# Three small changes at the hand-over from a dense stage to an expert stage: order of token-list loads, two more buffers for router rows, one group of matmuls moved

## The chip, the cores and the metric

The kernel runs on one core of one Trainium2 chip. The metric is the device time of one execution in microseconds (us). Engines: TensorE (PE, with its weight loads PEld), VectorE (DVE), ScalarE (ACT), GpSimd (POOL) and SyncE (SP), whose queue issues most DMAs; GpSimd issues the indirect ones.

## What is computed

Windowed causal attention (4 batches, 8 heads, 576 positions, head size 64), then a gated dense layer, then a top-1 routed layer of 8 experts. All is float32.

```python
attn = softmax(mask(q @ k.T / sqrt(D) + bias)); x = attn @ v        # 2304 tokens x 512
x = ((x @ w_a) * (x @ w_b)) @ w_out                                 # w_a, w_b: 512x1536, w_out: 1536x512
logits = x @ w_gate + modality_bias[modality_id]                    # 8 experts
e = argmax(logits); gate = max(softmax(logits))
out = gate * (relu(x @ w1[e]) @ w2[e])                              # w1[e]: 512x1024, w2[e]: 1024x512
```

## The kernel before

**Dense stage.** Tokens are cut into 18 tiles of 128 rows, in seven chunks of 3, 2, 2, 3, 3, 3 and 2 tiles (`CH`). A chunk runs 12 steps `j`; each has two accumulations of 12 matmuls (`mm_ab`, L503: `x @ w_a` and `x @ w_b`), the product of the two on DVE (`gf`, L1174), its split into two parts on ACT and DVE (`g`), and, one step later, the matmuls with `w_out` (`mm_out`, L520). Float32 accuracy comes from splitting each operand into a rounded part and a rest and adding three products. The order on PE, ACT and DVE is the written one in this stage (`tc.manual_schedule`); elsewhere a scheduler decides it.

**Router.** For chunks 2 to 5 the eight logits of a tile are taken on DVE during the next chunk: `rd_dot(e)` (L599) multiplies the three tiles of the chunk by row `e` of the gate matrix (`wgt`, 128x512, broadcast to all partitions, 256 KB) and sums (L602, tile `junk`). `rd_fetch(e)` (L594) asks for a row. There are two row buffers: rows 0 and 1 are asked for ahead of the chunk, row `e + 2` behind `rd_dot(e)`. For the last chunk (6), whose steps are `step6`, these dots run in its first eight steps. ACT and DVE have another duty in these steps: the first weights of the first expert unit (`un0`, a unit whose expert is known early) are loaded in quarters (`w1_load`, L893) and split (`w1_split`, L886 on ACT, L887 on DVE).

**Hand-over.** After the last chunk PE runs the first unit's first product (GEMM1, tile `ps_h`, L1282, 32 groups of three matmuls, each group one `yield` of `u_big`). Its groups are used to fill the gaps of a chain of small steps: transposes and logits of the last two tiles (`ps_x`, `ps_l`), their ranks (`ps_r`), the counts of tokens (`ps_c`, `ps_d`, `ps_e`) and the values `uv` that say which expert and which token list each later unit takes. The tables `AE` and `AD` say how many groups stand behind each of these steps: `AD[6]` first, then `AE` after each of the six parts of the last tiles' routing, then `AD[3]`, `AD[4]`, `AD[5]` behind `ps_c`, `ps_d`, `ps_e`, then all that is left.

**Expert stage.** Five units (`NFIX`) of 384 tokens follow for certain (`big(u)`), with one small unit inside the third. A unit's token list (`idx`, three columns of 128 numbers, a DMA of single numbers issued by SP, `u_idx`, L916) is needed by three indirect gathers on POOL (`xg`, L927), which bring 384 rows of 513 floats from the table `x2d`. PE transposes them (`ps_t`, L944), ACT and DVE split the result (`xT`). Eight weight quarters of 512 KB (`wr`: four of `w1`, four of `w2`) are asked for by SP through four buffers, and split by ACT and DVE into `w1s` and `w2s`. Then come GEMM1 (96 matmuls, `ps_h`) and GEMM2 (72 matmuls, `ps_y`, L1265). The scheduler places the transposes of a unit among the GEMM2 matmuls of the unit before. SP issues in order, and so does POOL.

Here unit 0 of this loop is called U0; the unit ahead of it, which runs GEMM1 in the hand-over and GEMM2 behind it, is called UE. In the code before, the lists of U0 and the four units behind it are asked for ahead of U0's weights.

Of the kernel before, what the change touches and what calls it, by code (L numbers as in the profile page):

```python
# [7 lines left out]
F32 = mybir.dt.float32  # L8
# [8 lines left out]
P = 128  # L17
# [4 lines left out]
def attn_moe_moe2(ctx: ExitStack, tc, q, k, v, moe_w_a, moe_w_b, moe_w_out, modality_id,  # L22
                  w_gate, w_gate_t, modality_bias, w1, w2, out):
    nc = tc.nc
    N, DM = out.shape
    DFF = moe_w_out.shape[0]
    E = w_gate.shape[1]
# [28 lines left out]
    m1 = ctx.enter_context(tc.tile_pool(name="m1", bufs=2))  # L56
# [54 lines left out]
    RG = N + 3 * P  # L111
    UT = 3 * P
    NSLOT = N // UT
    NS = E * NSLOT
    NFIX = N // UT - 1
    HT = P // 2
    NBIG = 11
# [314 lines left out]
    def wab_load(j):  # L432
        r = wab_p.tile([P, 2, KD, P, 2], U32, tag=f"wab{j}", name=f"wraw{j}")
        for m, w in enumerate((moe_w_a, moe_w_b)):
            nc.sync.dma_start(out=r[:, m].rearrange("p k f t -> p (k f t)"), in_=w.bitcast(U32)[j])
        wraw[j] = r
# [25 lines left out]
    def wo_load(j):  # L462
        r = m1.tile([P, DM, 2], U32, tag="wo", bufs=WOB, name="wor")
        mark["wo"] = nc.sync.dma_start(out=r.rearrange("p a b -> p (a b)"),
                                       in_=moe_w_out.bitcast(U32)[j * P:(j + 1) * P, :]).ins
        wraw["o", j] = r
# [122 lines left out]
    wgt = {}  # L589
# [3 lines left out]

    def rd_fetch(e):  # L594
        if not wgt:
            wgt[0] = m1.tile([P, 2, DM], F32, tag="ff", bufs=1, name="wgt")
        nc.sync.dma_start(out=wgt[0][:, e % 2], in_=w_gate_t[e:e + 1].partition_broadcast(P))

    def rd_dot(e):  # L599
        for i, x2, lgr in now:  # L600
            junk = m1.tile([P, DM], F32, tag="x2T", bufs=1, name="junk")
            nc.vector.tensor_tensor_reduce(out=junk, in0=x2[:, 0:DM], in1=wgt[0][:, e % 2], scale=1.0, scalar=0.0,  # L602
                                           op0=ALU.mult, op1=ALU.add, accum_out=lgr[:, e:e + 1])
        if e + 2 < E:
            rd_fetch(e + 2)

    def rd_step(j):
        if now and DJ <= j < DJ + E:
# [49 lines left out]
    @hp  # L658
    def a_loads(g):
        while pos["load"] < len(plist) and first[plist[pos["load"]]] <= g:  # L660
            c, hp = plist[pos["load"]]
            pairs[c, hp] = a_load(c, hp)
            pos["load"] += 1
# [216 lines left out]
    def ld(tile_, col, hi):  # L880
        return nc.values_load(tile_[0:1, col:col + 1], engines=SP, min_val=0, max_val=hi,
                              skip_runtime_bounds_check_because=WHY)

    def split(dst, srcw, early=False):
        if not early:
            nc.scalar.copy(out=dst[:, 0], in_=srcw)  # L886
            nc.vector.tensor_tensor(out=dst[:, 1], in0=srcw, in1=dst[:, 0], op=ALU.subtract)  # L887
            return
        for k in range(srcw.shape[1]):
            nc.scalar.copy(out=dst[:, 0, k], in_=srcw[:, k])  # L890
            (nc.gpsimd if k < W2P else nc.vector).tensor_tensor(out=dst[:, 1, k], in0=srcw[:, k], in1=dst[:, 0, k], op=ALU.subtract)

    def w1_load(ev, pool, f):  # L893
        r = pool.tile([P, KD, 2 * P], F32, tag="wr", name="wr1")
        nc.sync.dma_start(out=r.rearrange("p k f -> p (k f)"), in_=w1[bass.ds(ev, 1), f].rearrange("o p x -> p (o x)"))
        return r

    def w1_split(r):
        t = w1p.tile([P, 2, KD, 2 * P], F32R, tag="w1", name="w1s")
        split(t, r)  # L900
        return t

    def u_w1(ev, pool):
        return [w1_split(w1_load(ev, pool, f)) for f in range(4)]

    def u_w2(ev, pool, early=False):
        W2 = []
        for f in range(4):
            r = pool.tile([P, 2, DM], F32, tag="wr", name="wr2")
            nc.sync.dma_start(out=r.rearrange("p k f -> p (k f)"),  # L910
                              in_=w2[bass.ds(ev, 1), f].rearrange("o p x -> p (o x)"))
            t = w2p.tile([P, 2, 2, DM], F32R, tag="w2", name="w2s")
            split(t, r, early)
            W2.append(t)
        return W2

    def u_idx(ov, nt, pool, tag="idx", bufs=2):
        idx = pool.tile([P, 3], I32, tag=tag, bufs=bufs, name="idx")
        nc.sync.dma_start(out=idx[:, :nt], in_=tab[bass.ds(ov, nt * P), 0:1].rearrange("(t p) o -> p (t o)", p=P))
        return idx  # L920
# [232 lines left out]
    def evac(c):  # L1153
        for _ in evac_out(c):
            pass
        tr[:] = [[0, r] for r in tr]
        now.extend(rd)
        rd.clear()
# [46 lines left out]
    for c in range(NC):  # L1205
        n = CH[c] * P
        for j in range(NJ):
            if c == 0:
                if j == 0:
                    pe.enter_context(tc.manual_schedule(engines={  # L1210
                        mybir.EngineType.PE, mybir.EngineType.Activation, mybir.EngineType.DVE}))
                if j == 0:
                    wab_load(4)
                if j != 1:
                    wo_load(max(j, 1))
                if 0 < j < NJ - 4:
                    with tc.issue_after(mark["wo"]):
                        wab_load(j + 4)
                if j == CJ:
                    with tc.issue_after(mark["pt"]):  # L1220
                        consts_b()
                a_loads(goal[j] + LDA)
                pend, sc, tp = step0(j, pend, sc, tp) if j else step00()
                continue
            if j == 0:
                if c == NC - 1:
                    assert not sc and not tp and cur["s"] == len(items)
                    at_st.close()
                    w1p = ctx.enter_context(tc.tile_pool(name="w1p", bufs=4, side="right"))
                    wrp = ctx.enter_context(tc.tile_pool(name="wrp", bufs=1, side="right"))  # L1230
                    xgp = ctx.enter_context(tc.tile_pool(name="xgp", bufs=1, side="right"))
                if c - 1 in RD:
                    rd_fetch(0)
                    rd_fetch(1)
                mm_out(*pend, *([wo_t[NJ - 1]] if c == 1 else []))
                pend = None
                if c == 1:
                    evac(c - 1)
            if c > 1:
                wo_fetch(j, c)  # L1240
            if c < NC - 1:
                a_loads(goal[c * NJ + j] + LDA)
                if c == 3 and (j == 5 or j > 5 and zr):
                    x2_init()
                pend, sc, tp = step(c, j, pend, sc, tp)
                continue
            pend = step6(j, pend)
# [5 lines left out]
    m2 = ctx.enter_context(tc.tile_pool(name="m2", bufs=1))  # L1253
# [41 lines left out]

    fin = ExitStack()
    fin.enter_context(tc.manual_schedule(engines={mybir.EngineType.PE}))
    AD = [0,0,0,3,4,5,5]
    AE = [2,2,2,3,4,2]
    mm_out(*pend)  # L1300
    adv(AD[6])
    for a, _ in zip(AE, evac_out(NC - 1)):
        adv(a)
# [4 lines left out]
    nc.tensor.matmul(ps[:NS, 0:1], lhsT=os6.rearrange("p m e -> p (m e)"), rhs=ones[:, 0:1], start=True, stop=True)  # L1308
    adv(AD[3])
    un = rt.tile([P, 16], F32, tag="un", bufs=1, name="un")  # L1310
# [10 lines left out]
    nc.tensor.matmul(ps2[:NS, 4:7], lhsT=ones[:NS, :NS], rhs=ab[:NS, 0:3], start=True, stop=True)  # L1321
    adv(AD[4])
    nc.vector.tensor_copy(out=u_[:, 4:7], in_=ps2[:NS, 0:3])
# [20 lines left out]
    nc.tensor.matmul(ps3[0:1, :], lhsT=onef[:NS], rhs=vt[:NS], start=True, stop=True)  # L1344
    adv(AD[5])
    uv = const.tile([1, NV + 4], I32, name="uv")
# [89 lines left out]
            out=out, out_offset=bass.IndirectOffsetOnAxis(ap=idx, axis=0),  # L1436
            in_=y[0:HT], in_offset=None, bounds_check=N - 1, oob_is_err=False))

    S_A, S_B, S_C = 20, 29, 4

    def big(u, after=None, cont=None):
        ev = ld(uv, u, E - 1)
        pool = side()
        idx, xg = u_gather(*((None, 3, pool, idxs[u]) if u < NFIX else (ld(uv, NBIG + u, E * RG - UT), 3, pool)))
        W1, W2 = u_w1(ev, wrq), u_w2(ev, wrq)
        if after is not None:
            gs = small_load(after)
        xT = u_xT(xg, 3, pool, m_bank)
        for n_, _ in enumerate(u_big(idx, xg, xT, W1, W2, m_bank, FO and u != NFIX - 1)):
            if after is not None and n_ in (S_A, S_B):  # L1450
                next(gs)
            if cont is not None and n_ == S_C:
                next(cont, None)
        return gs if after is not None else None
# [6 lines left out]
    def small(u):  # L1461
        for _ in small_load(u):
            pass


    idxs = [u_idx(ld(uv, NBIG + u, E * RG - UT), 3, m2, f"idx{u}", 1) for u in range(NFIX)]
    gs = None
    for u in range(NFIX):
        gs = big(u, 0 if u == SAT - 1 else None, gs)
# [61 lines left out]
```

## Time and profile before

| | us |
|---|---|
| median of 3 runs (829.09 to 830.67) | 829.64 |
| the profiled execution: its own time | 828.1 |
| its span, first to last instruction | 826.4 |
| PE busy in the span | 800.0 (97%) |
| PEld, DVE, ACT, POOL busy | 721.9, 546.0, 460.7, 231.8 |

A row of the time-ordered view gives the start, the length, the engine, the line, the operation with its output and inputs, and in brackets how long the engine stood idle before it and who released it. Names are those of the program, without buffer numbers.

### The profile page before, as it was taken

Reading aid. Unit: us, or ns where it says so; the run is one execution under the profiler, and the core shown is the slowest. Engines: PE = TensorE matmul, PEld = TensorE weight load, DVE = VectorE, ACT = ScalarE, POOL = GpSimd, SP = SyncE. Lnnn points to the kernel's source line nnn. Section 1 sums busy time; section 2 is a strip of 40 time slices with the busy share of each in tenths; the row PEclk is TensorE's granted clock in tenths of the full one; section 3 lists DMA queues with packets and bytes.
Section 4 is the critical chain, followed back from the end, with each engine's and each line's share of the span. In section 5 each row is a group of like instructions: output and inputs, shape, how many; then the busy total and the mean of one; then the engine's idle time right before and its main releaser. Section 6 shows DMA issues by size and latency. Waiting matters only on the chain.

```text
span 826.4 us, 14380 instructions
## 1 busy us (share of the span) xinstructions
PE 800.0 (97%) x4686; PEld 721.9 (87%) x4686; DVE 546.0 (66%) x1571; ACT 460.7 (56%) x1161; POOL 231.8 (28%) x365
## 2 busy tenths in 40 slices
PE   9979999999999999999999999999998999999994
PEld 6857877998999999999999999989987998989893
DVE  7789997777666776668777776378746444446510
ACT  7755547877778766676667643223526444557420
POOL 5324261433243322342223322020422030303101
PEclk9999999999999999999999999999999999999997
DMA  9956646677556866555556444475438554638301
GB/s 244 372 197 213 231 139 194 216 225 228 172 161 176 224 170 171 143 152 144 158 149 170 126 134 121 132 228 206 142 104 278 194 182 131 214 92 316 120 14 41
DMA packets 78629, 145.13 MB, mean 176 GB/s; under 512 B 14095, under 2 KB 41903, under 8 KB 78544
## 3 DMA queue, kind: packets, MB, share of 16 engines
q1 hardware_dynamic: 74992, 134.39, 53.5%
q0 software_dynamic: 3552, 9.73, 3.3%
q8 instruction: 39, 0.64, 0.3%
q14 instruction: 46, 0.38, 0.1%
HBM read 118.16 MB, written 22.12 MB: 170 GB/s over the span
## 4 chain that ended last, share of the span: by engine, by line
PE 57%; issue 16%; DVE 11%; ACT 8%; DMA 4%; POOL 3%; SPq 0%; POOLq 0%; ACTq 0%
PE ps_ab L503 27%; PE acc L520 10%; PE ps_h L1282 5%; PE ps_y L1265 3%; PE acc L516 3%; PE ps_o L378 2%; PE ps_s L258 2%; ACT p L282 2%; PE ps_p L310 1%; POOL out L1272 1%; DVE f64f L426 1%; POOL xg L927 1%; DVE junk L602 1%; DMA xg<-x2d,idx 1%; DMA wgt<-in_wgt 1%
## 5 line engine op out<-in xcount | busy, mean ns | idle before, releaser
L503 PE MATMUL ps_ab<-xr,wab 128*128 128x384 f32 (+1 forms) x2016 | 326.5, 316 | 3.1 <-DVE gf L1174 1.3
L503 PEld LDWEIGHTS ps_ab<-xr,wab 128*128 128x128 f32 x2016 | 307.1, 188 | 14.9 <-issue 4.3
L520 PE MATMUL acc<-wo,g 128*128 128x512 f32 x540 | 135.3, 393 | 0.0
L326 POOL TENSOR_SCALAR_AFFINE_SELECT pt<-pc 128x512 fp32r<-128x512 f32 (+1 forms) x72 | 46.6, 647 | 268.6 <-DVE pc L324 243.8
L520 PEld LDWEIGHTS acc<-wo,g 128*128 128x128 f32 x540 | 96.9, 188 | 16.8
L1282 PE MATMUL ps_h<-xT,w1s 128*128 128x384 f32 x576 | 104.4, 337 | 0.0
L1265 PE MATMUL ps_y<-w2s,h 128*128 128x512 f32 x432 | 104.3, 396 | 0.0
L1282 PEld LDWEIGHTS ps_h<-xT,w1s 128*128 128x128 f32 x576 | 99.8, 188 | 0.9
L1265 PEld LDWEIGHTS ps_y<-w2s,h 128*128 128x128 f32 x432 | 80.7, 190 | 15.8
L282 ACT ACTIVATE p<-p,mx 128x128 f32<-128x128 f32 x144 | 56.8, 395 | 29.6 <-DVE mx L272 29.4
L602 DVE CUSTOM_DVE_ANT_0 junk<-x,wgt 128x512 f32<-128x512 f32 x88 | 62.0, 704 | 4.2 <-DMA wgt<-in_wgt 2.2
L387 ACT COPY u<-ps_o 64x384 f32<-64x384 f32 x120 | 56.8, 473 | 7.6 <-PE ps_o L378 6.2
L1272 POOL DMA_INDIRECT out<-y,idx x18 | 20.1, 1116 | 138.2 <-ACT y L1271 136.9
L301 ACT ACTIVATE p<-p,mx 128x128 f32<-128x128 f32 x120 | 41.8, 395 | 26.4 <-DVE mx L290 26.2
L1116 ACT CAST g<-gf 128x384 fp32r<-128x384 f32 (+1 forms) x60 | 28.2, 470 | 50.5 <-DVE gf L1114 50.0
L1117 DVE TENSOR_TENSOR g<-gf,g 128x384 fp32r<-128x384 f32 (+1 forms) x60 | 30.3, 505 | 37.7 <-ACT g L1116 37.7
L887 DVE TENSOR_TENSOR w2s<-wr,w2s 128x1024 fp32r<-128x1024 f32 x24 | 29.4, 1225 | 36.8 <-ACT w2s L886 35.8
L1114 DVE TENSOR_TENSOR gf<-ps_ab,asb 128x384 f32<-128x384 f32 (+1 forms) x60 | 30.2, 503 | 32.6 <-PE ps_ab L503 24.2
L887 DVE TENSOR_TENSOR w1s<-wr,w1s 128x1024 fp32r<-128x1024 f32 x28 | 34.2, 1224 | 23.4 <-ACT w1s L886 22.3
L1285 ACT ACTIVATE h<-ps_h 128x384 fp32r<-128x384 f32 x48 | 23.5, 491 | 40.8 <-PE ps_h L1282 38.7
L328 POOL TENSOR_SCALAR_AFFINE_SELECT pt<-pc 128x512 fp32r<-128x512 f32 (+1 forms) x72 | 46.3, 642 | 0.0
L1286 DVE SCALAR_TENSOR_TENSOR h<-ps_h,h 128x384 fp32r<-128x384 f32 x48 | 26.3, 554 | 24.9 <-ACT h L1285 24.8
(218 smaller groups left out, 1204.9 us busy)
## 6 DMA issues: line engine op xcount, KB each, us to landing
wo<-wo_d SPq DMA_DIRECT2D x60, 512.0 KB
wr<-in_moe_w SPq DMA_DIRECT2D x56, 512.0 KB
wgt<-in_wgt SPq DMA_DIRECT2D x32, 256.0 KB
wraw<-in_moe_w_a SPq DMA_DIRECT2D x12, 512.0 KB
wraw<-in_moe_w_b SPq DMA_DIRECT2D x12, 512.0 KB
wor<-in_moe_w_out SPq DMA_DIRECT2D x12, 512.0 KB
wo_d<-wo SPq DMA_DIRECT2D x12, 512.0 KB
kr<-in_k SPq DMA_DIRECT2D x24, 256.0 KB
```

The source lines that it names most:

```text
L282: nc.scalar.activation(out=it.p[:, h, :], in_=it.p[:, h, :], func=AF.Exp, bias=it.mx[:, 2 + h:3 + h], scale=-1.0, accum_out=it.mx[:, 4 + h ...
L301: nc.scalar.activation(out=it.p[:, h, :], in_=it.p[:, h, :], func=AF.Copy, scale=it.mx[:, 6 + h:7 + h])
L326: nc.gpsimd.affine_select(out=it.pt[:, :, 0], in_=pc, pattern=pat + [[-1, P]], base=0, channel_multiplier=1, compare_op=ALU.is_gt, fill=0.0)
L328: mark["pt"] = nc.gpsimd.affine_select(out=it.pt[:, :, 1], in_=pc, pattern=pat + [[1, P]], base=0, channel_multiplier=-1, compare_op=ALU.i ...
L387: nc.scalar.copy(out=u[o:o + 64], in_=it.po[o:o + 64, 1 - h:4 - h])
L503: nc.tensor.matmul(ps[:, :n], lhsT=w[:, m, r, kk * P:(kk + 1) * P], rhs=xr[:, s, kk, :n], start=(idx == 0), stop=(idx == len(terms) - 1))
L520: nc.tensor.matmul(acc[c, t], lhsT=g[:, r, t * P:(t + 1) * P], rhs=w[:, s, :], start=(j == 0 and idx == 0), stop=(j == NJ - 1 and idx == 2))
L602: nc.vector.tensor_tensor_reduce(out=junk, in0=x2[:, 0:DM], in1=wgt[0][:, e % 2], scale=1.0, scalar=0.0, op0=ALU.mult, op1=ALU.add, accum_ ...
L887: nc.vector.tensor_tensor(out=dst[:, 1], in0=srcw, in1=dst[:, 0], op=ALU.subtract)
L1117: nc.vector.tensor_tensor(out=gt[:, 1, :n], in0=gf[:, :n], in1=gt[:, 0, :n], op=ALU.subtract)
L1265: nc.tensor.matmul(pss[t], lhsT=h[:, r, f, t * P:(t + 1) * P], rhs=W2[f // 2][:, s_, f % 2, :], start=(f == 0 and i == 0), stop=(f == 7 an ...
L1282: nc.tensor.matmul(ps, lhsT=W1[f // 2][:, r, kk, (f % 2) * P:(f % 2 + 1) * P], rhs=xT[:, s_, kk, :], start=(kk == 0 and i == 0), stop=(kk ...
```

## The change

1. `rd_fetch` and `rd_dot` take the row buffers from a dictionary, and in the last chunk two more are added (`w6`, in a pool that opens on the space of the attention buffers when these close). So four rows are asked for at the start of that chunk, and row `e + 4` behind `rd_dot(e)`.
2. `AE` goes from `[2,2,2,3,4,2]` to `[2,2,3,3,3,2]`; of `AD`, entry 4 goes from 4 to 5 and entry 5 from 5 to 4. The sums are the same.
3. The list of U0 is asked for alone; those of units 1 to 4 are asked for in `big(0)`, behind the requests for U0's eight weight quarters.
4. `S_B`, which says in which group of the third unit a part of the small unit is written, goes from 29 to 30.

```diff
     def rd_fetch(e):
         if not wgt:
-            wgt[0] = m1.tile([P, 2, DM], F32, tag="ff", bufs=1, name="wgt")
-        nc.sync.dma_start(out=wgt[0][:, e % 2], in_=w_gate_t[e:e + 1].partition_broadcast(P))
+            ff = m1.tile([P, 2, DM], F32, tag="ff", bufs=1, name="wgt")
+            wgt.update({0: ff[:, 0], 1: ff[:, 1]})
+        nc.sync.dma_start(out=wgt[e % len(wgt)], in_=w_gate_t[e:e + 1].partition_broadcast(P))
...
-        if e + 2 < E:
-            rd_fetch(e + 2)
+        if e + len(wgt) < E:
+            rd_fetch(e + len(wgt))
...
+                    w6 = xgp.tile([P, 2, DM], F32, tag="wgt", name="wgt")
+                    wgt.update({2: w6[:, 0], 3: w6[:, 1]})
                 if c - 1 in RD:
-                    rd_fetch(0)
-                    rd_fetch(1)
+                    for e in range(max(2, len(wgt))):
+                        rd_fetch(e)
...
-    AD = [0,0,0,3,4,5,5]
-    AE = [2,2,2,3,4,2]
+    AD = [0,0,0,3,5,4,5]
+    AE = [2,2,3,3,3,2]
...
-    S_A, S_B, S_C = 20, 29, 4
+    S_A, S_B, S_C = 20, 30, 4
...
         W1, W2 = u_w1(ev, wrq), u_w2(ev, wrq)
+        if u == 0:
+
+            lists(range(1, NFIX))
...
-    idxs = [u_idx(ld(uv, NBIG + u, E * RG - UT), 3, m2, f"idx{u}", 1) for u in range(NFIX)]
+    idxs = {}
+
+    def lists(us):
+        for u in us:
+            idxs[u] = u_idx(ld(uv, NBIG + u, E * RG - UT), 3, m2, f"idx{u}", 1)
+
+    lists((0,))
```

**SP, start of the last chunk.** The three stores of the chunk before to the table, then the loads of `w_out` parts. Before:

```order
L561 DMA x2d<-x_6257 128x513
L483 DMA wo<-wo_d 128x1024 x4
L881 TENSOR_LOAD uv_663
L919 ISA
L919 DMA idx<-tab 128x3x1
L881 TENSOR_LOAD uv_663
L895 ISA
L895 DMA wr_7255<-in_moe_w 128x1024
L483 DMA wo<-wo_d 128x1024
L597 DMA wgt<-in_wgt 128x512
```

After:

```order
L561 DMA x2d<-x_6257 128x513
L598 DMA wgt<-in_wgt 128x512 x2
L483 DMA wo<-wo_d 128x1024 x4
L882 TENSOR_LOAD uv_663
L920 ISA
L920 DMA idx<-tab 128x3x1
L882 TENSOR_LOAD uv_663
L896 ISA
L896 DMA wr_7258<-in_moe_w 128x1024
L483 DMA wo<-wo_d 128x1024
L598 DMA wgt<-in_wgt 128x512
```

Two router rows (2 and 3) now stand ahead of the `w_out` loads; the next request, at the same place as before, is for row 4 where it was for row 2. The last two requests of the chunk are gone.

**SP, behind the counts.** `uv` names the unit's expert and list. Before, the fifth list, with four alike ahead of it, and then the first weight quarter:

```order
L881 TENSOR_LOAD uv
L919 ISA
L919 DMA idx<-tab 128x3x1
L881 TENSOR_LOAD uv
L895 ISA
L895 DMA wr_8315<-in_moe_w 128x1024
```

After, the first list is followed at once by the weights, and the other four stand behind the eighth quarter:

```order
L882 TENSOR_LOAD uv
L920 ISA
L920 DMA idx<-tab 128x3x1
L882 TENSOR_LOAD uv
L896 ISA
L896 DMA wr_8296<-in_moe_w 128x1024
```

Four list requests with their register loads have left the place between U0's list and its weights.

**PE, from the counts to the first product of U0.** Before:

```order
L1321 MATMUL ps_d<-ab,ones 48x3
L1282 MATMUL ps_h<-xT,w1s 128x384 x12
L1344 MATMUL ps_e<-vt,onef 1x40
L1282 MATMUL ps_h<-xT,w1s 128x384 x15
L1265 MATMUL ps_y<-w2s,h 128x512 x28
L944 MATMUL ps_t<-ident,xg 128x128 x4
L1265 MATMUL ps_y<-w2s,h 128x512
L944 MATMUL ps_t<-ident,xg 128x128 x4
L1265 MATMUL ps_y<-w2s,h 128x512 x42
L1282 MATMUL ps_h<-xT,w1s 128x384 x96
```

After:

```order
L1324 MATMUL ps_d<-ab,ones 48x3
L1285 MATMUL ps_h<-xT,w1s 128x384 x15
L1347 MATMUL ps_e<-vt,onef 1x40
L1285 MATMUL ps_h<-xT,w1s 128x384 x12
L1268 MATMUL ps_y<-w2s,h 128x512 x46
L945 MATMUL ps_t<-ident,xg 128x128 x4
L1268 MATMUL ps_y<-w2s,h 128x512 x6
L945 MATMUL ps_t<-ident,xg 128x128 x8
L1268 MATMUL ps_y<-w2s,h 128x512 x20
L1285 MATMUL ps_h<-xT,w1s 128x384 x96
```

One group of three stands ahead of `ps_e` now and not behind it. The transposes of U0's rows, in thirds of four, stand behind 46, 52 and 52 products of UE's GEMM2; they stood behind 28, 29 and 30. On ACT and DVE the splits of these transposes (`xT`) come after all four quarters of `w1` now, where they came after two. The change of `S_B` moves nothing on PE.

## Rows read from the trace of the kernel before

**Rows 1.** Stretches: busy us (count) of PE, PEld, DVE, ACT, POOL; clock, DMA share, GB/s
```profile
core 0: us, PE busy (x) PEld busy (x) DVE busy (x) ACT busy (x) POOL busy (x), PEclk, DMA share, GB/s
589.90:611.80 21.90, 21.08 (x130) 19.42 (x129) 16.26 (x69) 10.02 (x23) 8.15 (x7) 1.00 0.32 116
611.80:634.50 22.70, 19.44 (x86) 15.80 (x85) 9.77 (x11) 10.64 (x14) 4.92 (x5) 0.92 0.80 249
651.20:669.10 17.90, 17.90 (x86) 14.76 (x86) 7.51 (x9) 7.67 (x11) 0.31 (x1) 1.00 0.36 124
```
**Rows 2.** Time-ordered view, last chunk: SP, DVE, PE and ACT around a router row
```profile
520.21 1.51 SPq L561 DMA_DIRECT2D x2d<-x  x3
543.15 0.38 SPq L597 DMA_DIRECT2D wgt<-in_wgt  x1
547.19 0.42 SPq L597 DMA_DIRECT2D wgt<-in_wgt  x1
549.64 0.34 SPq L895 DMA_DIRECT2D wr<-in_moe_w  x1
555.08 0.69 DVE L602 CUSTOM_DVE_ANT_0 junk<-x,wgt 128x512 f32<-128x512 f32 x1 [2.16 <-DMA wgt<-in_wgt]
557.64 1.70 PE L503 MATMUL ps_ab<-xr,wab 128*128 128x256 f32 x12 [1.04 <-DVE gf L1174]
557.93 1.04 ACT L886 CAST w1s<-wr 128x1024 fp32r<-128x1024 f32 x1
562.23 0.42 DVE L1174 TENSOR_TENSOR gf<-ps_ab,asb 128x256 f32<-128x256 f32 x1
```
**Rows 3.** Time-ordered view, hand-over: the two waits of PE
```profile
598.00 1.06 PE L540 MATMUL ps_l<-wg,x2T 128*128 128x8 f32 x8 [0.37 <-ACT x2T L535]
608.94 0.23 PE L1344 MATMUL ps_e<-vt,onef 48*1 48x40 f32 x2 [0.45 <-DVE vt L1340]
```
**Rows 4.** Time-ordered view behind the counts: lists and weights on SP, gathers on POOL
```profile
609.95 3.93 SPq L919 DMA_DIRECT2D idx<-tab  x5
614.63 2.60 SPq L895 DMA_DIRECT2D wr<-in_moe_w  x4
612.61 0.97 POOL L927 DMA_INDIRECT xg<-x2d,idx  x1 [7.25 <-DMA idx<-tab]
615.15 0.95 POOL L927 DMA_INDIRECT xg<-x2d,idx  x1 [0.30 <-issue]
636.99 1.48 POOL L927 DMA_INDIRECT xg<-x2d,idx  x1 [0.30 <-issue]
638.77 0.97 POOL L927 DMA_INDIRECT xg<-x2d,idx  x1 [0.30 <-issue]
```
**Rows 5.** Time-ordered view, PE in GEMM2 of UE
```profile
619.57 0.66 PE L944 MATMUL ps_t<-ident,xg 128*128 128x128 f32 x4 [0.58 <-DMA xg<-x2d,idx]
623.15 1.12 PE L944 MATMUL ps_t<-ident,xg 128*128 128x128 f32 x4 [2.68 <-DMA xg<-x2d,idx]
```
**Rows 6.** Chain of waits, in order of time: start, us, what (GEMM1 of U0, then GEMM2)
```profile
634.69 16.67 PE ps_h L1282 x96
...
663.22 5.93 PE ps_y L1265 x26
```
**Rows 7.** One stretch of 1 us, columns as in rows 1
```profile
624.00:625.00 1.00, 1.00 (x5) 0.81 (x4) 0.79 (x2) 1.00 (x4) 0.00 (x0) 0.50 1.00 344
```
**Rows 8.** DMA view by stretch: 613.5:615, 617:623, 618:620, 547:554 (software = gathers): packets, MB
```profile
q0 software_dynamic: 26, 0.11, 49.5%
...
q1 hardware_dynamic: 454, 1.68, 75.5%
q0 software_dynamic: 143, 0.46, 24.5%
...
q0 software_dynamic: 25, 0.07, 9.7%
...
q0 software_dynamic: 266, 0.79, 36.2%
```

More of the change, by code (lines that the diff above doesn't have):

```diff
@@ L601, in rd_dot @@
             junk = m1.tile([P, DM], F32, tag="x2T", bufs=1, name="junk")
-            nc.vector.tensor_tensor_reduce(out=junk, in0=x2[:, 0:DM], in1=wgt[0][:, e % 2], scale=1.0, scalar=0.0,
+            nc.vector.tensor_tensor_reduce(out=junk, in0=x2[:, 0:DM], in1=wgt[e % len(wgt)], scale=1.0, scalar=0.0,
                                            op0=ALU.mult, op1=ALU.add, accum_out=lgr[:, e:e + 1])
-        if e + 2 < E:
-            rd_fetch(e + 2)
+        if e + len(wgt) < E:
+            rd_fetch(e + len(wgt))
     def rd_step(j):
```

## The prediction

> **What bounds the kernel now.** I read the table of engines first: PE is busy for 800.0 of 826.4 us, so the end is set by PE's work, and a change of order can win only where PE stands still or runs slowly. The table by slices and then the stretches show where that is. Between 611.8 and 634.5 PE does 86 matmuls in 22.70 us and is busy for 19.44 of them; between 651.2 and 669.1 it does the same mix, 86 matmuls, in 17.90 us without a gap [rows 1]. The first of these is GEMM2 of UE with the transposes of U0, the second GEMM2 of U0 with the transposes of the next unit. The time-ordered view names the wait: the second and third set of transposes wait 0.58 and 2.68 us for gathered rows [rows 5]. The stretch view adds a second loss. Right behind the wait the granted clock is 0.50, that is 1.2 GHz instead of 2.4, while PE is busy for the whole microsecond [rows 7]; ahead of it PE had stood from 620.5 to 623.15. So the slow stretch is part of the price of the wait: 22.70 - 17.90 = 4.8 us in all, 3.26 of it standing (22.70 - 19.44) and some 1.5 slow.
>
> Two smaller losses stand ahead of it. In the last chunk DVE waits 2.16 us for a router row, and PE then 1.04 us for `gf`, which stands behind that dot on DVE [rows 2]. In the hand-over PE waits 0.37 us for `x2T` and 0.45 for `vt` [rows 3].
>
> **Part 1, router rows.** The row that came too late was asked for at 547.19 and was there at 555.08, 7.9 us later [rows 2]. With four buffers it is asked for behind the stores of the chunk before, which are issued from 520.21 to 521.7, more than 30 us before its dot. Row 4 is then asked for at 543.15, where row 2 was, and its dot runs after 557, so it has 14 us where 7.9 were needed. The two early requests stand ahead of four loads of `w_out` on SP. They carry 0.5 MB and take two issue times of about 0.4 us [rows 2]; the loads behind them serve steps from 540 on, so 15 us and more hide this. The new buffers lie where the attention's buffers were, so the requests wait for the last attention work; the first `w_out` load behind that is issued before 522, and I cost the wait at nothing with the same cover. No bytes are added: eight rows before, eight after.
>
> What is late next? On ACT the split of a weight quarter (`w1s`, 557.93) follows. It was asked for at 549.64 [rows 2], and nothing shows when it landed. Its DVE half, three dots and the next `gf` (562.23) follow in order, and that `gf` is only just in time for PE now. For the whole 1.04 to stay won, the quarter must land by 556.9, 1.04 before the split's present start. By the 7.9 us of the router row it lands at 557.5, and 0.5 us are won; by its place in the queue, two requests and 0.5 MB behind the row that was there at 555.08, at 0.36 MB per us (2.14 MB from 617 to 623 [rows 8]), it lands at 556.5, and 1.04 are won. If it landed only at 557.9, nothing is won. I take **0.8**, between the two nearest, and keep 0 and 1.04.
>
> **Part 2, one group of matmuls.** A group is three matmuls at 16.67 / 96 = 0.17 us, or 0.52 us [rows 6]. One more stands ahead of the second `ps_l`, where PE waited 0.37, and one more ahead of `ps_e`, where it waited 0.45 [rows 3]; both are covered. Against it, one fewer stands ahead of the second tile's ranks and one fewer behind `ps_e`. The first takes 0.52 us of cover from DVE's steps for the second tile; at worst all of it comes back as a wait, and 0.82 - 0.52 = 0.3 are left. The second has the whole of GEMM2 behind it and costs nothing. I take **0.7**, since no wait of PE for these ranks shows in the trace; bounds 0.3 and 0.82.
>
> **Part 3, lists and transposes.** Before, SP issues five lists from 609.95 to 613.9 and the first weight quarter of U0 at 614.63 [rows 4]. Without four lists, at about 0.9 us each, the quarters start near 610.8. The first gather waits for its own list alone and stays at 612.61. The moved lists stand behind the eighth quarter, whose issue waits for the splits of the first four; the next unit's gathers started at 636.99 [rows 4], behind a scatter on POOL, so the list has some ten microseconds to spare, and SP's next work (the weights of the next unit) waits for buffers then anyway.
>
> What removes the wait is mainly the order on PE. GEMM2 of UE now starts one group earlier, 611.8 - 0.5 = 611.3. The first third of the transposes stands behind 46 products of 5.93 / 26 = 0.228 us [rows 6], at 611.3 + 10.5 = 621.8, and the last two thirds behind six more and four transposes, at about 623.7. Before, the last rows were there at 623.15 [rows 5], so even an unchanged landing is in time. But the landing does change: the weights now flow beside the gathers from their first byte, where they came two microseconds later.
>
> How long do the gathers take then? They move 384 x 513 x 4 bytes = 0.79 MB, and their first bytes show between 613.5 and 615 [rows 8], say 614.3. The gathers of UE, in a stretch with some weight traffic, moved their 0.79 MB in 7 us (547 to 554); beside U0's weights the same queue moved 0.46 MB in 6 us (617 to 623) [rows 8], which would make 10.3 us. So the last row lands between 621.3 and 624.6; the middle, 622.9, is ahead of 623.7. I take no wait, so the stretch takes the 17.90 us of its twin and **4.8** are won; at 624.6 PE waits 0.9 and 3.9 are won.
>
> Two rules of the Trainium skill bear on this. The rows show that the gather queue got 143 packets against 454 of the weights from 617 to 623 [rows 8]. DMA: Bandwidth & Descriptors, section Queues, rings and completion order, says that a DMA engine serves its queue rows in turn, a packet each; by even turns the gathers would get about half of 0.36 MB per us and land near 618.7. The trace does not agree that far, and its shares stand in the sum. The other speaks against the change. A gather issued at 636.99, beside a weight split on DVE, took 1.48 us on POOL, the next 0.97 [rows 4]. SBUF — State Buffer, section SBUF: two separate sides, says that a VectorE operation with two SBUF inputs can hold a port pair that GpSimd then waits for. By it the first splits of U0, which now come earlier, delay the third gather (615.15) by up to 0.5 us; the slow bound becomes 625.1, the wait 1.4, and the sum 0.5 lower there.
>
> The change of `S_B` moves nothing on PE; nothing.
>
> **Sum.** 0.8 + 0.7 + 4.8 = 6.3 us. The profiled execution took 828.1 us (826.4 and 1.7 around it), so it would be 821.8; it stands 1.5 under the median of 829.64, from which I subtract the same: **823.3 us**.
>
> **Rivals.**
> - *The gathers get thin beside the weights* (0.15): they land between 624.6 and 627, PE waits 1 to 3.3 us, and the clock falls again in the longer cases. For it speaks that the gather queue's share fell to 0.07 MB in 2 us from 618 to 620 [rows 8]; against it that these were the worst two microseconds. At 627 all of the 4.8 is back (3.3 standing, 1.5 slow): 829.6 - 1.5 = 828.1. The case runs from 824.3 to 828.1.
> - *The router row's wait is taken over by the weight quarter* (0.10): it lands at 557.9, part 1 gives nothing, 829.6 - 5.5 = 824.1. For it speaks the 7.9 us of the row asked just before.
> - *The gathers starve, and the kernel gets slower* (0.05): at 0.035 MB per us, the rate of 618 to 620 [rows 8], 0.79 MB take 22.5 us and land at 636.8; PE waits 13.1, the slow clock adds 1.5, and this loss of 14.6 stands where 4.8 was: 829.6 + 9.8 - 1.5 = 837.9. It decides from a landing at 630.2, a rate under 0.05: then the loss of 8.0 exceeds 4.8 + 1.5 by the 1.7 us that are 0.2%. Against it, the rate over 6 us was 0.077.
> - *The change does not do what it says* (0.03): U0's first product waits for something else, such as its weights, which are asked for in time before too: 829.6, no change.
>
> **How the numbers follow.** The forecast has 0.67 and reaches from 822.0 (all of 1.04, 0.82 and 4.8, and about 1 us for the spread of the runs) to 824.3. With most of the first rival and the second the range is 822.0 to 827.5; the starving case, no change, and the ends are left out. 0.2% is 1.7 us, about what a measurement can tell. Faster: 0.67 + 0.10 + 0.11 of the first rival = 0.88. Same: 0.03 + 0.04 = 0.07. Slower: 0.05.
>
> **What would show it.** In the new profile: no wait of DVE for `wgt`, and PE's 1.04 us gone, with no new wait for `gf` two steps later; no wait ahead of `ps_e`; the first weight quarter of U0 issued within 1.5 us of its list; no or under 1 us of wait ahead of U0's transposes, and a clock of 1.00 through GEMM2 of UE, which then takes about 18 us. I am wrong if transposes still wait by more than 1.5 us, if the slow clock stays without a wait, or if the won time comes back as a wait for weights in U0.

## Result, and the profile after

| | before | after |
|---|---|---|
| median of the runs (6 each, same chip) | 829.09 (828.71 to 830.67) | 821.36 (820.60 to 822.97) |
| ratio, 95% interval | | 0.9906 [0.9893, 0.9920] |
| the profiled execution: its own time / span | 828.1 / 826.4 | 821.9 / 820.1 |

The kernel is 7.7 us faster, about 1.4 us more than the forecast 6.3, and the median lies 0.6 us under the low end of the range. (The forecast, 823.3, is missed by 1.9 us: 1.4 are the gain, and 0.55 are the median of before, which is 829.64 in the three runs known then and 829.09 in six.) The two profiled executions differ by 6.3 us of span, just the forecast sum, but that is chance: by stages the profile shows more gained, and something else lost. The stretch view of the new kernel, with the columns of [rows 1], from the first matmul of the last chunk to that of GEMM1 of UE, on to GEMM2 of UE, and on to GEMM1 of U0:

```profile
core 0: us, PE busy (x) PEld busy (x) DVE busy (x) ACT busy (x) POOL busy (x), PEclk, DMA share, GB/s
536.20:589.60 53.40, 53.10 (x384) 49.45 (x383) 40.48 (x143) 17.27 (x42) 7.47 (x8) 1.00 0.60 187
589.60:610.70 21.10, 21.10 (x131) 19.51 (x130) 16.17 (x69) 10.05 (x23) 8.26 (x7) 1.00 0.34 122
610.70:628.40 17.70, 17.70 (x86) 14.71 (x85) 9.60 (x11) 10.54 (x14) 5.20 (x5) 1.00 0.91 311
```

The second and third answer to the two first of [rows 1]; the last chunk of the kernel before, in the same view:

```profile
534.40:589.90 55.50, 53.91 (x384) 49.70 (x383) 40.57 (x143) 17.06 (x42) 7.23 (x8) 1.00 0.58 190
```

From the starts to the hundredth, the last chunk goes from 55.51 to 53.43 us (2.08 won, forecast 0.8), the hand-over from 21.91 to 21.02 (0.89, forecast 0.7), GEMM2 of UE from 22.71 to 17.73 (4.98, forecast 4.8), and the rest from 191.87 to 191.71. That is 8.1 us won behind the start of the last chunk. But the chunk starts at 536.2 instead of 534.4: the other 1.8 us are lost far ahead of anything that was changed. The stretch from 50 to 75 us, before and after:

```profile
50.00:75.00 25.00, 21.61 (x94) 16.24 (x93) 23.05 (x41) 11.43 (x28) 9.03 (x12) 0.93 0.51 167
```
```profile
50.00:75.00 25.00, 21.19 (x84) 14.88 (x83) 21.40 (x38) 11.03 (x27) 8.47 (x12) 0.86 0.51 168
```

In both, PE stands at 56 to 59 us and the granted clock then falls from 1.00 to 0.50, from 2.4 to 1.2 GHz; how long it stays there differs, and ten matmuls fewer are done by 75 us in the new kernel. All thirteen traces of this study fall into two groups here: with a clock of 0.93 in these 25 us the last chunk starts between 534.3 and 535.2 us, with 0.86 between 535.8 and 536.9, whatever was changed later. So one profiled pair can mislead by some 2 us, and the stages are compared below from their own starts.

The last chunk in the time-ordered view, new kernel (SP, DVE, ACT, PE):

```profile
548.98 0.43 SPq L598 DMA_DIRECT2D wgt<-in_wgt  x1
551.43 0.34 SPq L896 DMA_DIRECT2D wr<-in_moe_w  x1
554.64 0.68 DVE L603 CUSTOM_DVE_ANT_0 junk<-x,wgt 128x512 f32<-128x512 f32 x1
556.82 2.98 PE L503 MATMUL ps_ab<-xr,wab 128*128 128x256 f32 x24
557.66 1.06 ACT L887 CAST w1s<-wr 128x1024 fp32r<-128x1024 f32 x1
558.75 1.23 DVE L888 TENSOR_TENSOR w1s<-wr,w1s 128x1024 fp32r<-128x1024 f32 x1 [0.71 <-ACT w1s L887]
574.94 2.98 PE L503 MATMUL ps_ab<-xr,wab 128*128 128x256 f32 x24
```

The dot that waited 2.16 us and the 24 matmuls that stood 1.04 us in their middle [rows 2] now run without a wait. Three steps of the chunk became shorter, not one. Where 24 matmuls now take 2.98 us each time, two later groups of the kernel before read:

```profile
561.21 3.20 PE L503 MATMUL ps_ab<-xr,wab 128*128 128x256 f32 x24
...
574.69 3.34 PE L503 MATMUL ps_ab<-xr,wab 128*128 128x256 f32 x24
```

These carry no bracket, since the idle pieces inside a group are too short to open a new row; the lag shows in the length of the group. From start to start the three steps are 1.33, 0.21 and 0.52 us shorter.

The hand-over and GEMM2 of UE, with the lists, weights and gathers (PE, then SP and POOL):

```profile
597.86 1.06 PE L540 MATMUL ps_l<-wg,x2T 128*128 128x8 f32 x8
608.29 0.23 PE L1347 MATMUL ps_e<-vt,onef 48*1 48x40 f32 x2
610.66 10.59 PE L1268 MATMUL ps_y<-w2s,h 128*128 128x512 f32 x46
621.09 0.60 PE L945 MATMUL ps_t<-ident,xg 128*128 128x128 f32 x4
622.93 1.04 PE L945 MATMUL ps_t<-ident,xg 128*128 128x128 f32 x8
```
```profile
609.31 0.39 SPq L920 DMA_DIRECT2D idx<-tab  x1
610.27 2.22 SPq L896 DMA_DIRECT2D wr<-in_moe_w  x4
623.70 3.38 SPq L920 DMA_DIRECT2D idx<-tab  x4
614.41 0.95 POOL L928 DMA_INDIRECT xg<-x2d,idx  x1 [0.30 <-issue]
629.55 1.01 POOL L1275 DMA_INDIRECT out<-y,idx  x1 [5.38 <-DMA idx<-tab]
630.87 1.46 POOL L928 DMA_INDIRECT xg<-x2d,idx  x1 [0.30 <-issue]
```

The waits of [rows 3] and [rows 5] are gone, and the clock is 1.00 through GEMM2. The four moved lists are issued at 623.70, and the next unit's gathers start at 630.87, 2.48 us behind the end of this GEMM2, and 2.46 before (636.99 behind 634.53). So the moved lists cost nothing, but they are only just in time. The first of them lands 5.7 us after its request, at 629.42, and the profile puts the end of POOL's wait before UE's last scatter (629.55) down to it. That scatter still starts 0.27 us behind the end of its `y` on ACT, as in e3 (0.28), and the gathers follow it. The list is there 1.5 us before the first gather, not the ten or so that were forecast.

### The profile page after: what moved, and what is told of

Its sections match the earlier page's. It is cut to its first block, busy times and chain, and to the rows that moved or that the text cites. A ratio compares the mean times of both kernels' runs of the same rounds, so it can differ in the third digit from the quotient of the medians.

```text
span 820.1 us, 14379 instructions
## 1 busy us (share of the span) xinstructions
PE 798.8 (97%) x4686; PEld 721.0 (88%) x4686; DVE 545.6 (67%) x1571; ACT 461.0 (56%) x1161; POOL 232.5 (28%) x365
## 4 chain that ended last, share of the span: by engine, by line
PE 58%; issue 15%; DVE 12%; ACT 8%; POOL 3%; DMA 2%; POOLq 0%; SPq 0%; ACTq 0%; DVEq 0%
PE ps_ab L503 26%; PE acc L520 10%; PE ps_h L1285 6%; PE ps_y L1268 4%; PE acc L516 3%; PE ps_o L378 2%; PE ps_s L258 2%; ACT p L282 2%; PE ps_p L310 1%; POOL out L1275 1%; DVE junk L603 1%; DVE f64f L426 1%; PE ps_s L254 1%; POOL xg L928 1%; ACT g L1117 1%
```

## Experiments

Stages are measured from start to start as above. "Lag" is what DVE stood for a router row in that profile; "wait" what PE stood for gathered rows in GEMM2 of UE.

| kernel | lag | last chunk | hand-over | wait | GEMM2 of UE | rest |
|---|---|---|---|---|---|---|
| before | 2.16 | 55.51 | 21.91 | 3.26 | 22.71 | 191.87 |
| after | 0 | 53.43 | 21.02 | 0 | 17.73 | 191.71 |
| e1, rows alone | 0 | 53.22 | 21.96 | 3.00 | 22.74 | 191.63 |
| e2, groups alone | 0.99 | 54.33 | 21.14 | 3.10 | 22.63 | 191.69 |
| e3, lists alone | 1.33 | 54.64 | 21.91 | 0 | 17.72 | 191.92 |
| e4, old lists, late transposes | 1.50 | 54.80 | 23.61 | 0 | 17.68 | 191.58 |
| e5, three row buffers | 0 | 53.76 | 21.15 | 0 | 17.73 | 191.60 |
| e6, after without lists | 0 | 53.20 | 21.96 | 3.95 | 23.30 | 191.55 |
| e7, e6 with late transposes | 0 | 53.26 | 20.98 | 0 | 17.68 | 191.61 |
| e8, after with three more dots | see there | 55.48 | 21.52 | 0 | 17.72 | 191.50 |

**e1, part 1 alone.** The kernel before with the `wgt` hunks of the change.

```diff
...
+                    w6 = xgp.tile([P, 2, DM], F32, tag="wgt", name="wgt")
+                    wgt.update({2: w6[:, 0], 3: w6[:, 1]})
                 if c - 1 in RD:
-                    rd_fetch(0)
-                    rd_fetch(1)
+                    for e in range(max(2, len(wgt))):
+                        rd_fetch(e)
```

> Part 1 alone (four router rows in the last chunk). My theory: the 2.16 us that VectorE stood for its second router row reached TensorE in three places of the chunk, not only in the one wait of 1.04 us; the 24 products that opened at 555.03, 561.21 and 574.69 in the kernel before shorten by about 1.3, 0.2 and 0.5 us, the chunk from its first product of A and B to the first product of GEMM1 goes from 55.5 to about 53.4, and the run is about 2.1 us shorter (ratio 0.9975). Rival, the prediction's own size: only the wait of 1.04 goes, 0.8 us in the end (ratio 0.999).

Measured: 826.37 us, ratio 0.9969 [0.9953, 0.9985], so 1.2 to 3.9 us faster; the chunk takes 53.22. My theory holds for the size, and the three places are the ones named. Its 2.1 us need care: they were drawn from the one trace in which the row was latest.

**e2, part 2 alone.**

```diff
-    AD = [0,0,0,3,4,5,5]
-    AE = [2,2,2,3,4,2]
+    AD = [0,0,0,3,5,4,5]
+    AE = [2,2,3,3,3,2]
```

> Part 2 alone (one group of products moved behind the first eviction of L and E). My theory: from the first product of GEMM1 to that of GEMM2 of the unit run in the hand-over 21.9 goes to about 21.0 us; the third gather, asked for by the lists as before, lands no earlier, so the transposes in front of GEMM2's end still wait for it and the 0.9 us are partly or wholly taken back there: between 0 and 0.9 us shorter in all. Rival, the parts simply add: 0.9 us shorter, and the wait for the third gather keeps its 2.7 us.

Measured: 827.42 us, ratio 0.9980 [0.9968, 0.9992], so 0.7 to 2.7 us faster. The hand-over is 0.77 us shorter, GEMM2 of UE no longer (22.63), so the parts add; that the 0.8 us would be taken back at the transposes was wrong. The gathers start from the same chain of counts and came that much earlier too: the third was waited for until 11.40 us behind the start of GEMM2, and 11.33 before.

**e3, part 3 alone.**

```diff
+        if u == 0:
+
+            lists(range(1, NFIX))
...
-    idxs = [u_idx(ld(uv, NBIG + u, E * RG - UT), 3, m2, f"idx{u}", 1) for u in range(NFIX)]
+    idxs = {}
...
+    lists((0,))
```

> Part 3 alone (token lists of units 1 to 4 asked for behind the first unit's weights). My theory: GEMM2 of the unit run in the hand-over goes from 22.7 to about 17.8 us, without a wait for gathered rows and at a granted clock of 1.00 throughout; the run is about 4.9 us shorter (ratio 0.994), and with parts 1 and 2 the three sum to some 7.9 us against 7.7 measured for all at once. Rival: part 3 leans on parts 1 or 2 (the third gather is in time only since the others moved), and alone it gives 3 us or less.

Measured: 823.33 us, ratio 0.9928 [0.9913, 0.9943]; GEMM2 of UE takes 17.72 us at a clock of 1.00. It does not lean on the other parts. The stages' gains sum to 2.1 + 0.9 + 5.0 = 8.0 against 7.7 measured. By the times the three parts alone sum to 10.2 us (2.6, 1.7 and 6.0), each uncertain by 1.0 to 1.2 us; in the profiles of e2 and e3 the late row also happened to land some 1 us earlier than in that of the kernel before. So it is the stages that show that the parts add, and the times are too coarse for it.

**e4, the place of the transposes alone.** Lists as in the kernel before, but U0's transposes behind the 52nd product of GEMM2 of UE (`yq` is the list of these products).

```diff
...
-        xT = u_xT(xg, 3, pool, m_bank)
+        if u == 0:
+            with tc.issue_after(yq[51]):
+                xT = u_xT(xg, 3, pool, m_bank)
+        else:
+            xT = u_xT(xg, 3, pool, m_bank)
```

> The kernel before, its lists asked for in the old order, but the first unit's transposes placed behind the 52nd product of GEMM2 instead of the 31st. If it is the place of the transposes that pays (the gathers land at 615 to 623.2 us as before, and the 52nd product ends near 623.8), TensorE no longer stands 2.68 and 0.58 us for them, the clock stays at 1.00 and the run is 4 to 5 us shorter as with part 3. If the earlier requests pay (gathers and weights), TensorE will wait again at the moved transposes or, next, for the first unit's xT copies or weights, and less than 2 us is gained.

Measured: 823.88 us, ratio 0.9937 [0.9922, 0.9952]. GEMM2 of UE takes 17.68 us with the lists and the weights asked for in the old order: the place of the transposes alone gives the whole of part 3, and the earlier requests add nothing that can be seen. The reverse, the lists moved and the transposes at their old place, was not run. But the landings tell against a gain from it: in the changed kernel the three gathers land 8.3, 9.7 and 10.9 us behind the start of GEMM2, and the old place, behind 28 to 30 products, comes after 6.4 to 6.9 us. In the kernel before, the second was waited for until 7.75 us and the third until 11.33, so with the weights asked for earlier the last gather landed 0.4 us earlier and the first two later. PE in this kernel:

```profile
597.35 1.26 PE L540 MATMUL ps_l<-wg,x2T 128*128 128x8 f32 x8 [0.51 <-ACT x2T L535]
598.46 3.19 PE L1283 MATMUL ps_h<-xT,w1s 128*128 128x384 f32 x9
...
612.74 11.95 PE L1266 MATMUL ps_y<-w2s,h 128*128 128x512 f32 x52
624.53 1.47 PE L944 MATMUL ps_t<-ident,xg 128*128 128x128 f32 x12
```

The twelve transposes run at 624.53 without a wait. In the hand-over this execution took 1.7 us more than that of the kernel before: nine matmuls of GEMM1 that take 1.84 us elsewhere take 3.19 behind a wait of 0.51. The stretch view of it, with the clock at 0.50:

```profile
599.00:600.00 1.00, 1.00 (x5) 1.00 (x4) 0.96 (x10) 0.58 (x3) 0.00 (x0) 0.50 0.00 0
```

**What the lag costs.** The four kernels with two row buffers asked for the late row in the same order, and its dot could start 7.9, 6.8, 7.1 and 7.3 us after the request (before, e2, e3, e4). DVE's wait in three of them (e2, e3, e4), against 2.16 in [rows 2]:

```profile
555.94 0.69 DVE L602 CUSTOM_DVE_ANT_0 junk<-x,wgt 128x512 f32<-128x512 f32 x1 [0.99 <-DMA wgt<-in_wgt]
```
```profile
555.65 0.69 DVE L602 CUSTOM_DVE_ANT_0 junk<-x,wgt 128x512 f32<-128x512 f32 x1 [1.33 <-DMA wgt<-in_wgt]
```
```profile
554.34 0.69 DVE L602 CUSTOM_DVE_ANT_0 junk<-x,wgt 128x512 f32<-128x512 f32 x1 [1.50 <-DMA wgt<-in_wgt]
```

Take the lag from the length of the chunk: 55.51 - 2.16 = 53.35, 54.33 - 0.99 = 53.34, 54.64 - 1.33 = 53.31, 54.80 - 1.50 = 53.30, and without lag it takes 53.2 to 53.4. For lags of 1 to 2.2 us, every microsecond of lag on DVE is a microsecond of the chunk. e8 tests whether that is DVE's pace or the transfers.

**e8, the lag without the wait.** The changed kernel with the dots of row 3 run twice in the last chunk, which gives the same sums.

```diff
+        if e == 3 and len(wgt) == 4:
+            for i, x2, lgr in now:
+                junk = m1.tile([P, DM], F32, tag="x2T", bufs=1, name="junk")
+                nc.vector.tensor_tensor_reduce(out=junk, in0=x2[:, 0:DM], in1=wgt[e], scale=1.0, scalar=0.0,
+                                               op0=ALU.mult, op1=ALU.add, accum_out=lgr[:, e:e + 1])
```

> The changed kernel with the three dots of row 3 run twice in the last chunk: three more operations of 0.69 and 0.08 us on VectorE, about 2.2 us, at the place where it stood 2.16 us in the kernel before, and no wait for any row. My theory, that VectorE sets the pace there and hands on any lag one for one: the chunk takes 55.5 us, TensorE waits about 1 us for gf at the same place, and all is 2.2 us slower than the changed kernel. Rival, the prediction's size: VectorE has 1.1 us of slack there, and the chunk grows by about 1.1 us. Second rival, the loss came from the transfers and not from VectorE's lag: no change.

Measured: 822.59 us, ratio 0.9931 [0.9904, 0.9959]; the interval is too wide to price it by the time, so the profile decides: the chunk takes 55.48 us, 2.05 more than in the changed kernel and 2.2 more than in e1, e6 and e7. DVE's next `gf` and PE's wait for it:

```profile
557.04 0.42 DVE L1180 TENSOR_TENSOR gf<-ps_ab,asb 128x256 f32<-128x256 f32 x1
```
```profile
557.52 1.68 PE L503 MATMUL ps_ab<-xr,wab 128*128 128x256 f32 x12 [1.02 <-DVE gf L1180]
```

The old picture is back, bracket of 1.02 included, with no late transfer. DVE sets the pace of these steps and has no slack in which to catch up; late transfers are not needed for the loss.

**e5, three row buffers.**

```diff
-                    w6 = xgp.tile([P, 2, DM], F32, tag="wgt", name="wgt")
-                    wgt.update({2: w6[:, 0], 3: w6[:, 1]})
+                    w6 = xgp.tile([P, 1, DM], F32, tag="wgt", name="wgt")
+                    wgt.update({2: w6[:, 0]})
```

> The changed kernel with three router row buffers in the last chunk instead of four. A row asked for at a dot then has two steps of the chunk, some 8 to 9 us, ahead of it, and in the four traces with two buffers so far a row landed 6.8 to 7.9 us after its request. My theory, that only the lag of the row counts: no wait of VectorE for a row, or one under 0.3 us, the chunk takes 53.3 us as with four, and the time is the same as the changed kernel's. Rival: the row that is asked for later runs against the weight quarter and still lags by 1 us; then the chunk takes 54.3 us.

Measured: 821.04 us, ratio 0.9902 [0.9875, 0.9928], as with four. No row is waited for; one buffer more than before would have done. The chunk takes 53.76, and what lag is left is in DVE's wait for the split of the weight quarter:

```profile
558.73 1.23 DVE L888 TENSOR_TENSOR w1s<-wr,w1s 128x1024 fp32r<-128x1024 f32 x1 [1.00 <-ACT w1s L887]
```

In e1 and e7 this wait is 0.52 us, which is what ACT's half of the split costs DVE there in any case; here it is 0.48 longer, in the changed kernel (0.71) 0.19. By the rule above these should give 53.2 + 0.48 = 53.7 and 53.4, and they do: 53.76 and 53.43.

**e6, the changed kernel without part 3.** Lists as in the kernel before; transposes behind the 31st product.

```diff
...
-    lists((0,))
+    idxs = [u_idx(ld(uv, NBIG + u, E * RG - UT), 3, m2, f"idx{u}", 1) for u in range(NFIX)]
```

> The changed kernel without its third part: lists asked for in the old order, the first unit's transposes behind the 31st product of GEMM2. My theory: parts 1 and 2 stay won (chunk 53.3, GEMM1 to GEMM2 21.0 us), GEMM2 of the unit run in the hand-over takes 22.6 to 22.8 us again with a wait of about 3 us for gathered rows; some 2.4 to 3 us faster than the kernel before (ratio 0.997), 5 us slower than the changed one. Rival: what parts 1 and 2 win is lost again in that wait, so the stretch grows to over 23.5 us.

Measured: 826.37 us, ratio 0.9969 [0.9953, 0.9985], about 5 us slower than the changed kernel. The profile does not follow the expected numbers everywhere: part 1 stays (53.20), but the wait for gathered rows is longer (3.95), and part 2's gain is absent in this execution (21.96), where ACT made `x2T` later than the moved group covers:

```profile
598.85 1.06 PE L540 MATMUL ps_l<-wg,x2T 128*128 128x8 f32 x8 [0.50 <-ACT x2T L535]
...
623.90 1.12 PE L945 MATMUL ps_t<-ident,xg 128*128 128x128 f32 x4 [3.95 <-DMA xg<-x2d,idx]
```

So part 2 is a cover of half a microsecond against an arrival that varies by as much.

**e7, the same with late transposes.** The edit of e4 on e6.

```diff
...
+        if u == 0:
+            with tc.issue_after(yq[51]):
+                xT = u_xT(xg, 3, pool, m_bank)
...
```

> The changed kernel without its third part, but the first unit's transposes placed behind the 52nd product of GEMM2. If the place of the transposes is all that pays in part 3, the stretch takes 17.7 us and the time is that of the changed kernel (ratio to before 0.991). If the earlier requests for weights and rows carry a part of it, a wait of 0.3 to 2 us stands at the transposes or ahead of U0's GEMM1 or GEMM2, and the kernel is that much slower than the changed one.

Measured: 820.71 us, ratio 0.9904 [0.9878, 0.9931]: the changed kernel's time without its third part.

**e9, e10, e11: how late is late enough, and what a wait costs.** e7 with the place moved.

```diff
-            with tc.issue_after(yq[51]):
+            with tc.issue_after(yq[46]):
```

(43 and 39 in e10 and e11.)

> As the run with late transposes and lists in the old order, but with U0's twelve transposes behind the 47th product of GEMM2 instead of the 52nd. The 47th ends 10.7 us after GEMM2's start; the third gather was there 11.1 to 12.3 us after it in the four runs that waited for it, so TensorE waits 0.4 to 1.5 us. The loss against the 52nd place is this wait alone if the slow clock needs a long stand; if any wait here brings the slow stretch of some 1.7 us, the loss is 2.1 to 3.2 us.

> The same with the transposes behind the 44th product, which ends 10.0 us after GEMM2's start: TensorE waits 1.1 to 2.3 us. With the slow stretch of some 1.7 us behind it the loss against the 52nd place is 2.8 to 4 us, without it 1.1 to 2.3.

> The same with the transposes behind the 40th product, 9.1 us after GEMM2's start: TensorE waits 2.0 to 3.2 us. With a slow stretch, as behind the waits of 2.7 to 4.0 us so far, the loss against the 52nd place is 3.7 to 4.9 us; without it 2.0 to 3.2.

| place | median, ratio to before | wait | GEMM2 of UE | over 17.68 | of that not standing |
|---|---|---|---|---|---|
| 52nd (e7) | 820.71, 0.9904 | 0 | 17.68 | | |
| 47th (e9) | 821.47, 0.9908 [0.9886, 0.9929] | 0.52 | 18.39 | 0.71 | 0.19 |
| 44th (e10) | 822.37, 0.9926 [0.9905, 0.9947] | 1.06 | 18.93 | 1.25 | 0.19 |
| 40th (e11) | 823.75, 0.9934 [0.9911, 0.9957] | 1.92 | 21.42 | 3.74 | 1.82 |
| 31st (e6) | 826.37, 0.9969 [0.9953, 0.9985] | 3.95 | 23.30 | 5.62 | 1.67 |
| 31st (e2) | 827.42, 0.9980 [0.9968, 0.9992] | 3.10 | 22.63 | 4.95 | 1.85 |

(e6 is the changed kernel at the old place; e2 has two row buffers, so its median is not to be held against the others.) PE's waits in e10 and e11:

```profile
621.13 1.31 PE L945 MATMUL ps_t<-ident,xg 128*128 128x128 f32 x10 [1.06 <-DMA xg<-x2d,idx]
```
```profile
622.45 1.40 PE L945 MATMUL ps_t<-ident,xg 128*128 128x128 f32 x10 [1.92 <-DMA xg<-x2d,idx]
```

And the stretch view behind them, first e10, then e11:

```profile
622.00:623.00 1.00, 1.00 (x9) 0.87 (x7) 0.15 (x1) 1.00 (x2) 0.00 (x0) 1.00 1.05 369
```
```profile
624.00:625.00 1.00, 1.00 (x4) 0.73 (x3) 0.45 (x1) 1.00 (x3) 0.00 (x0) 0.50 0.93 332
```

Behind waits of 0.52 and 1.06 us the clock stays at 1.00, and little beyond the wait is lost. Behind 1.92 it falls to 0.50, and 1.8 us come on top, about the same as behind 3.10 and 3.95. The expectation that any wait brings the slow stretch falls, for these two; but the wait of 0.51 us in e4's hand-over did bring it. Which short waits bring it was not settled.

No version beats the changed kernel by more than the runs spread; e5 (one row buffer fewer) and e7 (no list moved) are as fast with less.

## Why the prediction was right, and where wrong

**The step that failed is part 1's term**: "For the whole 1.04 to stay won ... I take 0.8 ... and keep 0 and 1.04". The row's wait was the right cause, but I bounded its price by the one bracketed wait of PE that followed it, as if the other 1.1 of DVE's 2.16 us had been absorbed. They were not: e8 and the four lags show that the chunk lengthens by all of DVE's lag. Of the 1.33 us in the first of the three steps 1.04 stand in the bracket; the other two steps add 0.21 and 0.52, in groups of 3.20 and 3.34 us that take 2.98 without the lag. In the profiled pair the term is 2.08 (2.16 by the rule), over the kernels with two buffers 1.0 to 2.2. My top bound of 1.04 was half the size, and with it the low end of the range, 822.0: with 2.1 in its place the sum is 7.6 and the forecast 822.0, and the low end would have been near 820.9. (In the working behind the 0.8 the gain for a landing at 557.5 is 557.9 - 557.5 = 0.4 and not 0.5; that moves the term by 0.05.)

What should have shown it in the trace of before: between 547 and 562 DVE never waits for PE; all its brackets name ACT or a transfer. An engine that never waits for the one it feeds is not ahead of it.

**The weight quarter** was "late next" in kind: it landed in time or up to half a microsecond late, and cost 0.19 us here and 0.48 in e5. The rival that it takes over the row's wait did not come.

**Part 2** was right: 0.89 against 0.7, and so just over its top bound of 0.82, both waits of [rows 3] gone, no new wait for ranks. e6 shows that the cover is thin. `S_B`, costed at nothing, shows next to nothing: the rest takes 191.5 to 191.7 us in the kernels with 30 and 191.6 to 191.9 in those with 29.

**Part 3** was right in size (4.98 against 4.8) and in its reason, "mainly the order on PE", which e4 and e7 change alone. The split of the 4.8 into 3.3 standing and 1.5 slow holds too: 17.7 without either, some 1.8 us beyond the wait at 1.92, 3.10 and 3.95 us (the last 23.30 - 17.68 - 3.95 = 1.67). What the prediction made of the earlier requests was needless: with late transposes the gathered rows were there in time in the old order too. The forecast of their landing came out: the third gather was there 7.2 us after its issue at 614.41, at 621.6, the early end of the forecast 621.3 to 624.6. The two rivals on gathers getting thin did not come either. The "some ten microseconds to spare" for the moved lists were 1.5. The DMA view of the new kernel from 617 to 623 (hardware queue, then the software queue, with the gathers and a scatter of UE) stands against the rows of 143 packets and 0.46 MB [rows 8]:

```profile
q1 hardware_dynamic: 420, 1.52, 71.7%
q0 software_dynamic: 217, 0.69, 31.7%
```

The Trainium skill (DMA: Bandwidth & Descriptors, Queues, rings and completion order) has the queues served in turn, a packet each; with 420 against 217 the trace is nearer to that than before, and still not even; no row here shows whether the profile's packets are those of the page. The delay of U0's third gather by a split on DVE, which the prediction weighed from the Trainium skill (SBUF — State Buffer, SBUF: two separate sides), does not show: it took 0.95 us. That is no case against the rule, since the split beside it started at 614.89, 0.48 us behind the gather. Where a split did start first, it cost up to 1.0 us in the kernel before, twice what the prediction took for the most (last section).

**The time as a whole**: the causes named for all three parts were the right ones, part 1's path to PE was not, and the gain was 7.7 where 6.3 was forecast. By the stages of the profiled pair 1.3 of the 1.8 us above the sum are part 1's.

## What to carry to other kernels

Price a late input on the engine that waits for it, then ask whether that engine has slack before its consumer. Here it never waited for the consumer, the whole lag counted, and it showed downstream in groups that grew longer as much as in a bracketed wait. A wait for a gather in the middle of a long product went away here by placing the waiting work later among independent matmuls; seven places too early (the 40th instead of the 47th) cost three microseconds here, since the clock fell too. Compare stages from their own starts: an unrelated stretch that comes in two lengths can hide or fake two microseconds between two profiled executions.

## What the runs showed of the hardware that was not expected

- The loss behind a stand of PE came in steps, not in proportion: 0.19 us beyond waits of 0.52 and 1.06, and 1.7 to 2.1 beyond waits of 1.92 to 3.95. One wait of 0.51, in another place and kernel, brought the clock to 0.50 for three microseconds; waits of 0.34 to 0.50 at that same place in five other traces did not.
- The same load at the same place of the program let its dot start 6.8 to 7.9 us after the request in four executions, and the chunk's length followed, from 54.33 to 55.51 us.
- In the first chunk one and the same stand of PE (2.0 us for `p`) is followed by a slow stretch of either of two lengths (mean clock 0.93 or 0.86 from 50 to 75 us), in code that none of the kernels changes.
- A gather's instruction on POOL takes 0.9 to 1.0 us by itself, and up to 1.95 us where a split on DVE (`w1s` or `w2s`, 1.23 us) had started at least 0.1 us before it. In all thirteen traces it then ends 0.8 to 0.9 us after that split; a split that started behind the gather, as in U0's third (614.89 against 614.41 in the new kernel), did not lengthen it. The longest in the kernel before, DVE and then POOL:

```profile
708.90 1.23 DVE L887 TENSOR_TENSOR w1s<-wr,w1s 128x1024 fp32r<-128x1024 f32 x1 [1.87 <-ACT w1s L886]
709.01 1.95 POOL L927 DMA_INDIRECT xg<-x2d,idx  x1 [0.30 <-issue]
```
